# The last 64 queries of every batch taken apart: attention-times-V in 64-column tiles, in front of the next batch's scores

## The chip, the core and the metric

The kernel runs on one core of one Trainium2 chip. The metric is device time in microseconds (us), the median of several executions; lower is better. The engines are named as in the profile: PE (TensorE matmul; PEld is its weight load), DVE (VectorE), ACT (ScalarE), POOL (GpSimd) and SP (SyncE, which here only issues DMAs).

## What is computed

The reference, cut to what matters (8 batches, 8 heads, 576 positions, head dimension 64; then 4608 tokens, width 512, hidden width 2048):

```
scores = q @ k.T / sqrt(64) + bias_table[bucket(i - j)]     # per batch and head, 576 x 576
attn   = exp(scores - max); attn /= sum(attn)
x      = attn @ v                                           # heads side by side: 4608 x 512
h      = x @ w_in                                           # 4608 x 2048
g      = h + sin(alpha * h)**2 / alpha
out    = g @ w_out                                          # 4608 x 512
```

The bias is constant beyond a distance of 128, so the kernel multiplies the exponentials by a table only in a band around the diagonal.

## The kernel before

**Tiling.** Heads go in pairs p = 0..3, pairs in groups g = 0, 1. Keys lie on the partitions: four blocks of 128 keys (c = 0..3) and a rest of 64 keys per head, which for the two heads of a pair are put into one block of 128 rows with zeros in the other head's half (`kts`, `vhs`). The 576 queries run along the free dimension: 512 and a last 64.

**Scores of a batch** (`plan_unit`, L644). A unit is one pair of PSUM banks and one exp on ACT (L678) that reads it. Kind A is one pair of heads, one key block, queries 0 to 511: two matmuls with 64 rows each, one per head, side by side in the array. Kind B is a group's last 64 queries against the four key blocks: 16 small matmuls of 64x64. Kind C is a pair's rest of keys against all 576 queries: two matmuls of 288 columns. The exps write the tile `u` (a group; two buffers); DVE multiplies the band of `u` by the table (L703, L687, L716). `plan_att` (L723) writes out a group's order by hand: A A A, C, A A A, C, A A B, for two groups; so a batch has six stretches of 64-row matmuls on PE and 22 exps on ACT.

**AV** (`plan_av`, L839), attention times V, for a pair: the weights are `u` (keys x 128 queries), the streamed operand is V with a column of ones (65 columns), whose result is the row sum. A query tile of 128 takes nine matmuls: one of 130 columns for the rest of keys (`vh`) and eight of 65 (two heads, four key blocks). From batch 1 on a pair has two windows (`WIN`, L287): queries 0 to 383 in three tiles, and 384 to 575 in two tiles that start at 384 and 448, so that 64 queries are computed twice. Then DVE takes the reciprocal of the sums and multiplies (L885, L886) into `xn`, and `xn` is transposed into `xT`: by a DMA transpose that SP issues (L898) for the first pairs (all but the last from batch 2 on), by PE and a copy (L910, L917) for the others. From batch 2 on that is five PE transposes a batch.

**Batch 0** is special: its windows are 256, 256 and 64 queries (`WIN0`, L288), and its last 64 queries are done in batch 1: `plan_late` (L777) makes the B units into a tile `ut`, and `plan_tail` (L792) the AV with weights of 64 columns, two pairs side by side in the array, 18 matmuls per group. POOL copies the rest-of-keys part of `u` into `ut` (L690).

**The second half**, per block b of 512 tokens: `plan_moe_in` (L926) makes 16 tiles h (four matmuls of 512 columns each, "w_in" below), sin on ACT (L950), a square on ACT or DVE (L957, L959), and on DVE the sum that gives g (L964). `plan_mo` (L996) multiplies g by w_out: four groups of 16 matmuls of 512 columns ("w_out" below), each group in one PSUM bank (6 or 7), copied to `outs` by DVE or ACT (L537, L539) and stored by an SP DMA (L1018). Block b starts when the queries it needs of batches b-1 and b are in `xT`. Exp and sin need different ACT tables, so there are two table loads a batch (L1025).

**The order.** `Plan.run` (L148) is a planner that runs while the kernel is built: each task has an engine, a cost, a priority and dependencies, and the planner emits the task that can start first. The 64 w_out matmuls of a block are its filling: they have the lowest priority (`fill`) and go where PE would wait, up to a quota during the scores (`QUOTA`, L211). On the chip each engine runs its own stream in the emitted order and waits by semaphores. PSUM banks 0 to 5 go to scores (in pairs), h and transposes; 6 and 7 to AV and w_out.

Of the kernel before, what the change touches and what calls it, by code (L numbers as in the profile page):

```python
# [32 lines left out]
D_TBL = 1.285  # L33
LAT = {"PE": 0.2, "ACT": 0.18, "DVE": 0.18, "POOL": 0.2, "SP": 2.4}
NBUF = {"u": 2, "g": 2, "s16": 3, "sq": 3, "outs": 5, "xn": 6}
# [175 lines left out]
QUOTA = 48  # L211
QUOTA1 = 44
# [4 lines left out]
T_KEEP = 20.0  # L217
# [14 lines left out]
T_LD = 33.0  # L232
AV0 = 1200
# [31 lines left out]
def kernel(  # L265
# [21 lines left out]
    WIN = ((0, 384), (384, 192))  # L287
    WIN0 = ((0, 256), (256, 256), (512, 64))  # L288
# [72 lines left out]
    def new_u():  # L361
        return tp.tile([128, 2, 9, S], F16, name="u", tag="u", bufs=NBUF["u"])

# [162 lines left out]
    ut = nat1x[:, 0 : NP * 9 * 64].rearrange("p (h k q) -> p h k q", h=NP, k=9)  # L526
    utb, udone = Buf("ut"), {}
# [116 lines left out]
    def plan_unit(t, g, p, kind, c, u, ub, done, gate, base):  # L644

        b, sc, mark = Buf("sc"), Cell(), plan.add({}, None)
        y = p - 2 * g
        b.users.append(mark)

        def qk(e):  # L650
            sc.v = bank(b, 2)
            kT, qT = kTs[t % 2], qTs[t % 2]
            if kind == "C":
# [13 lines left out]

        def ex(e):
            if kind == "A":
                o = u.v[:, y, 0:8, :].rearrange("p (z c) q -> p z c q", z=2)[:, :, c, 0:512]  # L670
                x = sc.v
            elif kind == "B":
                o = u.v[:, :, 0:8, 512:S] if t else ut[:, 2 * g : 2 * g + 2, 0:8, :]
                x = sc.v.rearrange("p z (c y q) -> p y (z c) q", c=4, y=2)
            else:
                o = u.v[:, y, 8, :].rearrange("p (b q) -> p b q", b=2)
                x = sc.v[:, :, 0:288]
            nc.scalar.activation(out=o, in_=x, func=AF.Exp, scale=0.125)  # L678

        n = 576 if kind == "C" else 1024  # L680
        x = plan.add({"ACT": n / 1200.0 + 0.065}, ex, [mark] + gate, base + 20, use=[b, ub])
        late = 0.0 if t else T_MH if kind == "C" else T_M2[p]
        if kind == "C":

            def bd(e):
                io = u.v[:, y, 8, 384:S]
                k_of(e).tensor_tensor(out=io, in0=io, in1=mh[:, p, 0:192], op=ALU.mult)  # L687

            def keep(e):
                nc.gpsimd.tensor_copy(out=ut[:, p, 8, :], in_=u.v[:, y, 8, 512:S])  # L690

            done[(p, "C", 0)] = x
            d = done[(p, "C", 1)] = plan.add(
                {"POOL": 0.6} if t == 0 and p else {"DVE": 0.19}, bd, [x], base + 10, nb=late, use=[ub])
            if t == 0:
                udone[(p, "C")] = plan.add({"POOL": 0.25}, keep, [d], base + 10, nb=T_KEEP, use=[ub])
# [13 lines left out]
        else:  # L710

            def bd(e):
                io = u.v[:, :, 0:8, 512:S] if t else ut[:, 2 * g : 2 * g + 2, 0:8, :]
# [4 lines left out]
            d = plan.add({"DVE": 0.25}, bd, [x], base + 10, nb=late, use=[ub])  # L718
            for pp in (2 * g, 2 * g + 1):
                done[(pp, "B", 0) if t else (pp, "B")] = d  # L720
        return b, mark, qk, x

    def plan_att(t, g, gates, first, gate):  # L723
# [6 lines left out]
        if t == 0:  # L730
            runs = [[x] for r in runs for x in r if x[1] != "B"]
        exps, head = [], []
        n_run = 0
        for i, units in enumerate(runs):
            base = PB + 3200 * g + (600 * i if t else 300 * i)
            made = [plan_unit(t, g, *x, u, ub, done, gate, base + 30 * k)
                    for k, x in enumerate(units)]
            deps = list(gates)
            for p, kind, _ in units:
                for pp in ((a, b) if kind == "B" else (p,)):  # L740
                    if t < 2:
                        deps += tr[(t, pp, 0)][1 if kind == "C" else 0] + tr[(t, pp, 1)][0]

            def run(e, i=i, made=made):
                if i == 0:
                    if g == 0:
                        first()
                        plan.in_qk, plan.used = True, 0
                        plan.quota = QUOTA1 if t == 1 else QUOTA
                    u.v = new_u()  # L750
                plan.share = (g * len(runs) + i + 1) / (2 * len(runs))
                if g == 1 and i == len(runs) - 1:
                    plan.in_qk = False
                for x in made:
                    x[2](e)

            if units[0][1] == "C":
                d, ends = 0.245, [0.245]
            else:
                ends = [0.1 + 0.2185 * (k + 1) for k in range(len(units))]  # L760
                d = ends[-1] + 0.11
            m = plan.add({"PE": d}, run, deps, base, after=head,
                         new=([ub] if i == 0 else []) + [x[0] for x in made],
                         use=[] if i == 0 else [ub])
            m.pad = () if t else (256,)
            m.offs = ([0.0] if i == 0 else []) + [0.1 + 0.2185 * k for k in range(len(units))]
            m.marks = [(x[1], o) for x, o in zip(made, ends)]
            head = [m]
            exps += [x[3] for x in made]
        for p in (a, b):  # L770
            for w in range(2):
                i = (2, 4)[w] if p == a else 4
                base = PB + 3200 * g + 600 * i + 50 * w
                xdone.setdefault((t, w), []).extend(plan_av(t, g, p, w, u, ub, done, base))
        return exps

    def plan_late(base, gate):  # L777

        made = [plan_unit(0, g, 2 * g, "B", 0, None, utb, udone, gate, base + 30 * g) for g in range(2)]
# [5 lines left out]
        m = plan.add({"PE": 0.65}, run, pe_gate, base, new=[x[0] for x in made])  # L785
        m.offs = [0.1, 0.32]
        m.marks = [(x[1], o) for x, o in zip(made, (0.32, 0.54))]
        for g in range(2):
            plan_tail(g, base + 1200 + 100 * g)
        return [x[3] for x in made]  # L790

    def plan_tail(g, base):  # L792
        ab, xb, tb = Buf("av"), Buf("xn"), Buf("h")
        av, xn, tr_ = Cell(), Cell(), Cell()
        us = [udone[(2 * g + y, k)] for y in range(2) for k in "CB"]

        def mm(e):
            av.v = bank(ab)
            for k in range(9):
                for y in range(2):  # L800
                    p, r = 2 * g + y, slice(64 * y, 64 * y + 64)
                    if k == 0:
                        full(av.v[r, 0 : 2 * VC], ut[:, p, 8, :], vhs[0][:, p, :], True, False)
                        continue
                    z, c = (k - 1) // 4, (k - 1) % 4
                    full(av.v[r, VC * z : VC * z + VC], ut[:, p, 4 * z + c, :],
                         vs[0][:, c, 2 * p + z, :], False, k == 8)

        x = plan.add({"PE": 0.5}, mm, us, base, new=[ab], use=[utb])

        def norm(e):
            x = av.v[:, 0 : 2 * VC].rearrange("p (z d) -> p z d", z=2)
            xn.v, rd = new_xn(), new_rd()
            r = rd[:, 0:2]
            nc.vector.reciprocal(out=r, in_=x[:, :, D])
            nc.vector.tensor_tensor(
                out=xn.v[:, 0].rearrange("p (z d) -> p z d", z=2), in0=x[:, :, 0:D],
                in1=r.unsqueeze(2).to_broadcast([128, 2, D]), op=ALU.mult,
            )

        x = plan.add({"DVE": 0.47}, norm, [x], base, new=[xb], use=[ab])

        def turn(e):
            tr_.v = bank(tb).bitcast(F16)
            nc.tensor.transpose(out=tr_.v[:, 0:128], in_=xn.v[:, 0], identity=id_sb)

        x = plan.add({"PE": 0.06}, turn, [x], base, new=[tb], use=[xb])

        def put(e):
            copy_on(e, xT[:, 2 * g : 2 * g + 2, 512:S],  # L830
                    tr_.v[:, 0:128].rearrange("p (y q) -> p y q", y=2))

        xdone.setdefault((0, 2), []).append(plan.add(
            {"DVE": t_dve(128), "ACT": t_act(128) + 0.03}, put, [x], base, use=[tb]))

    QC = ((0, 128, 256), (384, 448))
    QC0 = ((0, 128), (256, 384))

    def plan_av(t, g, p, w, u, ub, done, base):  # L839

        q0, n = (WIN if t else WIN0)[w]
        QS = (QC if t else QC0)[w]
        nq = len(QS)
        y = p - 2 * g
        ab, xb, tb = Buf("h" if t == 0 and p == NP - 1 and w else "av"), Buf("xn"), Buf("h")
        av, xn = Cell(), Cell()
# [260 lines left out]
```

## Time and profile before

| | us |
|---|---|
| median of 3 runs (382.63 to 382.76) | 382.65 |
| the profiled execution's own time | 383.65 |
| its span, first to last instruction | 381.8 |
| PE busy, of the span | 373.5 |
| ACT busy | 313.5 |
| DVE busy | 266.9 |
| POOL busy | 92.9 |

The profile is of one execution. Its page gives busy times, a digit row per engine (40 equal slices of the span, busy share in tenths), the chain of work that ended last, and groups of equal instructions. The mean time of one matmul is a latency: matmuls are pipelined, so what one costs in a stream is the distance between starts, which the timeline shows. Batch 1's scores begin at 53.3 us, and from 77 us to 321 us the batches 2 to 7 repeat: from one set of three PE transposes to the next there are 41.5 us for the first of these periods and 40.5 to 40.6 us for each of the next five. The last stretch (from 321 us) holds two blocks of the second half.

### The profile page before, as it was taken

The numbers are of one execution on the slowest core, as the hardware profiler recorded it, in microseconds if no ns is written. First come the engines' busy times: TensorE is split into PE (matmuls) and PEld (weight loads), VectorE is DVE, ScalarE is ACT, GpSimd is POOL, SyncE is SP. The second block draws the span as 40 slices with busy tenths as digits, with TensorE's granted clock in tenths as the row PEclk, the third lists the DMA queues.
The fourth block names the chain that finished last, engine by engine and source line by source line (L and its number), as shares of the span: only waits on it lengthen the run. The fifth ranks groups of instructions, "written<-read, shape, count | busy, mean of one in ns | idle before, by whom it ended". The sixth has DMA issues, their size and how long they took to land.

```text
span 381.8 us, 8975 instructions
## 1 busy us (share of the span) xinstructions
PE 373.5 (98%) x3578; PEld 204.2 (53%) x3578; DVE 266.9 (70%) x590; ACT 313.5 (82%) x432; POOL 92.9 (24%) x136
## 2 busy tenths in 40 slices
PE   8899999999999999999999999999999999999995
PEld 4365445654465445785564456544677456444442
DVE  4496976769676967697668867796769676999000
ACT  2978999869997999799987999699979997998111
POOL 7477350046000550037000900073005000000000
PEclk9979999999999999999999999999999999999999
DMA  9989999299912999279927991699629522000212
GB/s 170 177 160 196 203 154 134 56 162 116 89 53 74 151 120 121 79 130 113 137 60 123 103 165 44 105 147 139 78 75 155 60 53 74 6 2 1 77 63 82
DMA packets 148106, 40.16 MB, mean 105 GB/s; under 512 B 136200, under 2 KB 142432, under 8 KB 148064
## 3 DMA queue, kind: packets, MB, share of 16 engines
q0 software_dynamic: 96032, 17.67, 57.3%
q1 hardware_dynamic: 51856, 21.84, 25.1%
q8 instruction: 28, 0.46, 0.5%
q14 instruction: 14, 0.11, 0.1%
q10 hardware_dynamic: 176, 0.09, 0.1%
HBM read 37.73 MB, written 16.56 MB: 142 GB/s over the span
## 4 chain that ended last, share of the span: by engine, by line
PE 89%; ACT 5%; DMA 2%; DVE 2%; issue 1%; ACTq 0%; DVEq 0%; SPq 0%
PE pb L454 89%; ACT s L950 2%; DMA m2r<-e_dram 1%; ACT u L678 1%; DMA e_dram<-e_sb 1%; ACT sq L957 1%; PE pb L910 1%; ACT qT L537 0%; DVE u L703 0%; DVE xn L886 0%; DVE sq L959 0%; DVE outs L539 0%; DVE kT L539 0%; DVE g L964 0%; ACT xT L537 0%
## 5 line engine op out<-in xcount | busy, mean ns | idle before, releaser
L678 ACT ACTIVATE u<-pb 128x1024 f16<-128x1024 f32 (+1 forms) x174 | 152.7, 962 | 12.8 <-PE pb L454 12.0
L454 PE MATMUL pb<-w_out,g 128*128 128x512 f16 x576 | 138.9, 380 | 0.2 <-DVE outs L539 0.2
L454 PE MATMUL pb<-xT,w_in 128*128 128x512 f16 (+4 forms) x704 | 127.7, 340 | 0.0
L950 ACT ACTIVATE s<-pb,alphaT 128x512 f16<-128x512 f32 x144 | 92.9, 685 | 15.4 <-PE pb L454 15.2
L964 DVE SCALAR_TENSOR_TENSOR g<-sq,inv_a,pb 128x512 f16<-128x512 f16 x144 | 101.3, 743 | 3.8 <-ACT sq L957 2.3
L454 PEld LDWEIGHTS <-w_in 128*128 128x128 f16 x704 | 64.1, 98 | 55.9
L703 DVE TENSOR_TENSOR u<-u,m2r 128x512 f16<-128x512 f16 (+1 forms) x128 | 62.4, 497 | 35.0 <-ACT u L678 31.4
L454 PEld LDWEIGHTS <-g 128*128 128x128 f16 x576 | 53.0, 98 | 60.1 <-issue 8.1
L454 PEld LDWEIGHTS <-u 128*128 128x128 f16 x1404 | 55.5, 99 | 10.9 <-issue 3.2
L454 PE MATMUL pb<-v,u 128*128 128x65 f16 x1248 | 55.3, 195 | 0.2 <-DVE u L703 0.2
L399 POOL COPY kt<-kT 64x256 f16<-64x256 f16 x12 | 5.6, 464 | 182.9 <-DMA kT<-staged_k 182.7
L454 PE MATMUL pb<-qT,kT 64*128 64x64 f16 (+1 forms) x512 | 42.8, 288 | 0.4 <-ACT u L678 0.2
L959 DVE TENSOR_TENSOR sq<-s 128x512 f16<-128x512 f16 x81 | 34.3, 425 | 11.1 <-ACT s L950 10.2
L957 ACT ACTIVATE sq<-s 128x512 f16<-128x512 f16 x63 | 39.8, 631 | 0.9
L454 PE MATMUL pb<-vh,u 128*128 128x130 f16 x156 | 34.9, 224 | 0.0
L886 DVE TENSOR_TENSOR xn<-pb,rd 128x256 f16<-128x256 f32 (+1 forms) x64 | 30.9, 482 | 2.4 <-DVE rd L885 0.3
L537 ACT ACTIVATE outs<-pb 128x512 f32<-128x512 f32 x15 | 9.0, 597 | 28.1 <-PE pb L454 28.1
L454 PEld LDWEIGHTS <-kT 64*128 64x128 f16 x512 | 16.7, 94 | 24.5 <-issue 16.6
L404 POOL DMA_DIRECT2D v<-in_v_dram x28 | 24.8, 898 | 4.7 <-DMA nat<-in_q_dram 2.4
L1025 ACT ACT_TABLE_LOAD x15 | 19.2, 1283 | 0.3
L885 DVE RECIPROCAL rd<-pb 128x4 f32<-128x4 f32 (+1 forms) x64 | 11.9, 185 | 10.8 <-PE pb L454 9.7
L539 DVE COPY outs<-pb 128x512 f32<-128x512 f32 x21 | 14.5, 689 | 4.1 <-PE pb L454 4.0
(77 smaller groups left out, 168.7 us busy)
## 6 DMA issues: line engine op xcount, KB each, us to landing
out_dram<-outs SPq DMA_DIRECT2D x36, 256.0 KB, 2.3
v<-in_v_dram POOLq DMA_DIRECT2D x28, 128.0 KB, 4.4
staged_k<-in_k_dram POOLq DMA_DIRECT2D x6, 576.0 KB, 8.2
staged_q<-in_q_dram POOLq DMA_DIRECT2D x6, 576.0 KB, 12.0
w_in<-in_moe_w_in_dram POOLq DMA_DIRECT2D x4, 512.0 KB, 7.8
w_out<-in_moe_w_out_dram POOLq DMA_DIRECT2D x4, 512.0 KB, 15.1
xT<-xn SPq DMA_TRANSPOSE x60, 2.3
w_out<-in_v_dram SPq DMA_DIRECT2D x6, 128.0 KB, 4.8
```

Of the source, the lines that this page charges most:

```text
L404: nc.gpsimd.dma_start(out=vs[t % 2][:, c, :, 0:D], in_=vp[128 * c : 128 * c + 128],)
L454: nc.tensor.matmul(out=out, lhsT=lhsT, rhs=rhs, start=start, stop=stop)
L539: k_of(e).tensor_copy(out=o, in_=i)
L678: nc.scalar.activation(out=o, in_=x, func=AF.Exp, scale=0.125)
L703: nc.vector.tensor_tensor(out=io, in0=io, in1=m2[:, 2 * p : 2 * p + 2, x0 : x0 + hi - lo], op=ALU.mult)
L885: nc.vector.reciprocal(out=r, in_=x[:, :, :, D])
L886: nc.vector.tensor_tensor(out=xn.v[:, 0:nq].rearrange("p c (z d) -> p c z d", z=2), in0=x[:, :, :, 0:D], in1=r.unsqueeze(3).to_broadcast([ ...
L950: nc.scalar.activation(out=s16.v, in_=h.v, func=AF.Sin, scale=alphaT[:, f : f + 1])
L957: nc.scalar.activation(out=sq.v, in_=s16.v, func=AF.Square)
L959: k_of(e).tensor_tensor(out=sq.v, in0=s16.v, in1=s16.v, op=ALU.mult)
L964: nc.vector.scalar_tensor_tensor(out=gcell[b].v[:, f, :], in0=sq.v, scalar=inv_a[:, f : f + 1], in1=h.v, op0=ALU.mult, op1=ALU.add,)
L1025: nc.scalar.preload_act_table_set(name)
```

## The change

All batches now do their last 64 queries as batch 0 did, with changes to where they are put.

- `u` has 512 queries instead of 576. The last 64 queries of a batch go into a tile `ut` of their own, one of two halves by the batch's parity.
- Kind C covers 512 queries, and from batch 1 on two pairs at once (two matmuls of 512 columns, one exp of 1024). A new kind X covers all pairs' rest of keys against the last 64 queries (four matmuls of 64 columns in one bank, one exp of 256).
- A batch's order from batch 1 on is written out over both groups (`plan_att`); it still has six stretches of 64-row matmuls, and 21 exps.
- AV of queries 0 to 511 is in a stretch of three tiles (0 to 383) per pair, and one tile (384 to 511) per pair, two pairs together in one bank, one normalization and one DMA transpose; there are no overlapping tiles. From batch 2 on only the last pair's three tiles are transposed by PE.
- AV of the last 64 queries of batch t-1 (36 matmuls with weights of 64 columns, for all four pairs, in one row) is emitted right ahead of the first scores of batch t, as part of the same task; for batch 0 in batch 1 and for batch 7 it is a task of its own (`tail_alone`).
- Constants: `QUOTA` 48 to 44, `QUOTA1` 44 to 32. POOL's copies into `ut` are gone.

The diff, cut to its core:

```diff
 def plan_unit(...):
+        two = kind == "C" and t > 0
+            if kind == "X":
+                for pp in range(NP):
+                    full(sc.v[:, 64 * pp : 64 * pp + 64], kts[t % 2][:, pp, :], qT[:, pp, 512:S], True, True)
+                return
             if kind == "C":
                 for z in range(2):
-                    full(sc.v[:, z, 0:288], kts[t % 2][:, p, :],
-                         qT[:, p, 288 * z : 288 * z + 288], True, True)
+                    if two:
+                        full(sc.v[:, z, :], kts[t % 2][:, p + z, :], qT[:, p + z, 0:512], True, True)
+                    else:
+                        full(sc.v[:, z, 0:256], kts[t % 2][:, p, :],
+                             qT[:, p, 256 * z : 256 * z + 256], True, True)
...
-    def plan_att(t, g, gates, first, gate):
-        runs = ([(a, "A", 0), (a, "A", 1), (a, "A", 2)], [(a, "C", 0)],
-                [(a, "A", 3), (b, "A", 0), (b, "A", 1)], [(b, "C", 0)],
-                [(b, "A", 2), (b, "A", 3), (b, "B", 0)])
+    def plan_att0(g, gates, gate):
...
+    def plan_att(t, gates, gate):
+        A = [(p, "A", c) for p in range(NP) for c in range(4)]
+        runs = (A[0:3], [(0, "C", 0)], A[3:6], A[6:9], A[9:12], [(2, "C", 0)], A[12:15],
+                A[15:] + [(0, "B", 0), (2, "B", 0)], [(0, "X", 0)])
...
+            tl = plan_tail(t - 1, base) if i == 0 and t > 1 else None
+            def run(e, i=i, made=made, tl=tl, fresh=fresh):
...
+                if tl:
+                    tl[0](e)
+                for x in made:
+                    x[2](e)
...
+        for p in range(NP):
+            plan_av(t, [(p, 128 * i) for i in range(3)], *us[p // 2], done, bases[(2, 3, 5, 7)[p]],
+                    p < (2, NP - 1)[t > 1])
+        for g in range(2):
+            ps = [[2 * g, 2 * g + 1]] if g == 0 or t > 1 else [[2], [3]]
+            for x in ps:
+                plan_av(t, [(p, 384) for p in x], *us[g], done,
+                        bases[(4, 7)[g]] + 50 if g == 0 or t == 1 else PB + AV_LATE, g == 0 or t > 1)
...
+    def tail_alone(t, base):
+        tl = plan_tail(t, base)
+        m = plan.add({"PE": D_TAIL + 0.1}, tl[0], tl[1], base, new=[tl[2]], use=[tl[3]])
...
-    def plan_tail(g, base):
+    def plan_tail(t, base):
         def mm(e):
             av.v = bank(ab)
-            for k in range(9):
-                for y in range(2):
+            for g in range(2):
+                x0 = 2 * VC * g
+                for k in range(9):
+                    for y in range(2):
+                        p, r = 2 * g + y, slice(64 * y, 64 * y + 64)
...
+        if t:
+            def turn(e):
+                for y in range(2):
+                    nc.sync.dma_start_transpose(
+                        out=xT[:, y::2, x0 : x0 + 64],
+                        in_=xn.v[64 * y : 64 * y + 64, 0:2].rearrange("p c d -> p (c d)"),
+                    )
...
+        if t == T - 1:
+            tail_alone(t, PB + 10015)
```

The emitted order of PE in a period changes with it (w_in is 64 matmuls, M counts w_out matmuls, A A A is six 64-row matmuls, v27 are three query tiles of AV, X a PE transpose, T36 the new set of 36, A B B one A and two B units):

```
before: w_in M12 AAA M3 C M8 AAA M3 C M2 v27 M2 AAB M9 AAA v27 C M5 v18 AAA M1 v18 C M3 v27 AAB M11 v27 M5 X3 v36 w_in(X2 after its first 8)
after:  w_in M17 T36 AAA M3 C M8 AAA M6 v27 AAA M9 AAA v27 C M4 v18 AAA M1 v27 M3 ABB M3 X-scores M3 v27 M6 X3 v18 M1 w_in
```

More of the change, by code (lines that the diff above doesn't have):

```diff
@@ L232 @@
 T_LD = 33.0
+AV_LATE = 9000
 AV0 = 1200
@@ L685, in bd @@
             def bd(e):
[L686 to L696, printed above, removed]
+                io = ut[:, :, 8, :]
@@ new lines, in bd @@
+                nc.vector.tensor_tensor(out=io, in0=io, in1=mh[:, :, 128:192], op=ALU.mult)
+            done["X"] = plan.add({"DVE": 0.25}, bd, [x], base + 10, use=[ub])
+        elif kind == "C":
+            ys = slice(0, 2) if two else slice(y, y + 1)
+            def bd(e):
+                io = u.v[:, ys, 8, 384:512]
+                k_of(e).tensor_tensor(
+                    out=io, in0=io, in1=mh[:, 2 * g + ys.start : 2 * g + ys.stop, 0:128], op=ALU.mult
+                )
+            d = plan.add({"POOL": 0.45} if t == 0 and p else {"DVE": 0.25 if two else 0.15}, bd, [x],
+                         base + 10, nb=late, use=[ub])
+            for pp in (p, p + 1) if two else (p,):
+                done[(pp, "C", 0)], done[(pp, "C", 1)] = x, d
@@ L753, in run @@
                     plan.in_qk = False
+                x[2](e)
+            d, ends = run_time([unit + (False,)])
+            m = plan.add({"PE": d}, run, deps, base, after=head,
+                         new=([ub] if i == 0 else []) + [x[0]], use=[] if i == 0 else [ub])
+            m.pad = (256,)
+            m.offs = ([0.0] if i == 0 else []) + [0.1]
+            m.marks = [(x[1], ends[0])]
+            head = [m]
+            exps += [x[3]]
+        for p in (a, b):
+            for w in range(2):
+                base = PB + 3200 * g + 600 * ((2, 4)[w] if p == a else 4) + 50 * w
+                plan_av(0, [(p, 256 * w), (p, 256 * w + 128)], u, ub, done, base, False)
@@ L754, in run @@
                 for x in made:
                     x[2](e)
[L757 to L765, printed above, removed]
@@ L766, in plan_att @@
-            m.offs = ([0.0] if i == 0 else []) + [0.1 + 0.2185 * k for k in range(len(units))]
-            m.marks = [(x[1], o) for x, o in zip(made, ends)]
+            d, ends = run_time([x + (True,) for x in units])
+            d0 = D_TAIL if tl else 0.0
+            m = plan.add({"PE": d0 + d}, run, deps + (tl[1] if tl else []), base, after=head,
+                         new=([tl[2]] if tl else []) + new + [x[0] for x in made],
+                         use=use + ([tl[3]] if tl else []))
@@ L781, in run @@
+        units = [(0, "B", 0), (2, "B", 0), (0, "X", 0)]
+        made = [plan_unit(0, *x, None, tb, done, gate, base + 30 * k) for k, x in enumerate(units)]
         def run(e):
@@ L783, in run @@
                 x[2](e)
[L785 to L789, printed above, removed]
-        return [x[3] for x in made]
-    def plan_tail(g, base):
+        m = plan.add({"PE": 0.78}, run, pe_gate, base, new=[tb] + [x[0] for x in made])
+        m.offs = [0.0, 0.1, 0.32, 0.6]
+        m.marks = [(x[1], o) for x, o in zip(made, (0.32, 0.54, 0.78))]
@@ L809, in plan_tail @@
[L809 to L834, printed above, removed]
@@ L905, in plan_av, with made @@
-        tr_, x1 = Cell(), QS[0]
+            xn.v = new_xn()
+            norm_av(av.v, xn.v, nq)
+        x = plan.add({"DVE": 0.4 + 128 * nq / 960.0}, norm, prev, base + (NORM_PRI if t else NORM0),
+                     new=[xb], use=[ab])
+        x0 = S * t % XN + q0
+        two = parts[-1][0] > p0
+        def made(x):
+            rows = S * t + q0, S * t + parts[-1][1] + 128
+            xdone.append((t, rows, p0, x))
+        if dma:
+            def turn(e):
+                o = (xT[:, p0 : p0 + 2, x0 : x0 + 128] if two else
+                     xT[:, p0, x0 : x0 + 128 * nq].rearrange("d (c q) -> d c q", c=nq))
+                nc.sync.dma_start_transpose(
+                    out=o, in_=xn.v[:, 0:nq].rearrange("p c d -> p (c d)"))
+            made(plan.add({"SP": 0.3}, turn, [x], base, use=[xb]))
+            return
@@ L1046 @@
                 tr[(0, p + 1, kq)] = plan_tr(0, p + 1, kq, (150, 650, 5)[p], T_PAIR[p][kq])
-        for g in range(2):
-            if t == 1 and g == 1:
+        if t == 0:
+            for g in range(2):
+                exps += plan_att0(g, pe_gate, gate)
+        else:
+            exps += plan_att(t, pe_gate, gate)
+            if t == 1:
                 exps += plan_late(PB + LATE, gate)
-            exps += plan_att(t, g, pe_gate, first, gate)
         if t == 0:
@@ L1066 @@
             plan.add({"SP": 5.5}, turn_in, [], PB + 9000, after=tbl + [
-                x for w in range(2) for x in xdone[(t, w)] if "SP" in x.engs])
+                x for tt, _, _, x in xdone if tt == t and "SP" in x.engs])
+        if t == T - 1:
+            tail_alone(t, PB + 10015)
         sins = []
```

258 lines of the change are left out of this document (153 added, 105 removed).

## The prediction, made before the changed kernel was run

> **What bounds the kernel now.** I read the page's busy times and slices first, then the chain of work that ended last, then busy time by stretch for the repeating batches.
>
> ```profile
> PE 373.5 (98%) x3578; PEld 204.2 (53%) x3578; DVE 266.9 (70%) x590; ACT 313.5 (82%) x432; POOL 92.9 (24%) x136
> PE   8899999999999999999999999999999999999995
> PE 89%; ACT 5%; DMA 2%; DVE 2%; issue 1%; ACTq 0%; DVEq 0%; SPq 0%
> ```
> ```profile
> 158.92:199.56 40.64, 40.64 (x452) 26.67 (x450) 30.70 (x68) 36.20 (x48) 10.34 (x11) 1.00 1.00 111
> 199.56:240.04 40.48, 40.48 (x389) 21.40 (x386) 30.60 (x68) 36.20 (x48) 10.31 (x11) 1.00 1.03 111
> ```
> In the second fence the first number after a stretch is its length; then come PE, PEld, DVE, ACT and POOL busy, the granted clock and the DMAs. PE is busy in all of it, at a granted clock of 1.00, ACT 36.2 us of 40.5. A busy PE can still hide small waits behind a pipelined matmul's latency; I take those from distances between starts, below. So a period is the sum of PE's stream plus PE's small waits. What PE issues less of comes off, as long as ACT (4.3 us idle a period) does not become the loop.
>
> **PE prices.** Distances between starts in the timeline:
>
> ```profile
> 53.33 0.82 PE L454 MATMUL pb<-qT,kT 64*128 64x512 f16 x6
> 54.08 0.25 PE L454 MATMUL pb<-vh,nat 128*64 128x130 f16 x2
> 54.16 0.42 PE L454 MATMUL pb<-v,nat 128*64 128x65 f16 x16
> 54.51 0.39 PE L454 MATMUL pb<-w_out,g 128*128 128x512 f16 x1
> ...
> 142.11 0.22 PE L454 MATMUL pb<-vh,u 128*128 128x130 f16 x1
> 142.16 0.41 PE L454 MATMUL pb<-v,u 128*128 128x65 f16 x8
> 142.41 0.22 PE L454 MATMUL pb<-vh,u 128*128 128x130 f16 x1
> ```
> An AV tile of nine matmuls costs 142.41 - 142.11 = 0.30 us. Batch 0's tail in the old kernel (18 matmuls with 64-column weights) took 54.51 - 54.08 = 0.43 us with the way out of that shape: the 2 of 130 columns 0.08, then eight pairs at 0.03 each, then 0.12 to the next matmul where 0.03 is the pair: 0.095 is the change of shape. The two of a pair start 0 to 7 ns apart, so they run side by side. The same 0.095 is at each change to and from the 64-row scores (w_out to scores 0.311 instead of 0.2155, and back 0.308 instead of 0.213).
>
> **The change on PE, part by part.**
> 1. AV tiles: batches 1 to 7 lose 4 of 20 tiles: 28 x 0.30 = -8.40 us.
> 2. Tails. A set of 36 streams 2 x (0.077 + 8 x 0.030) = 0.635. Ahead of scores it adds one change of shape (the change into the scores is there anyway): 0.73, six times. Batch 0's set lies between an A run and C and batch 7's among w_in: 0.82 each. The old tail of batch 0 cost 2 x 0.43 + 2 x 0.093 = 1.05. Together 6 x 0.73 + 2 x 0.82 - 1.05 = +4.97.
> 3. PE transposes: 58 before, 44 after by the built order; three take 0.17 (118.27 to 118.44 in the timeline), so 14 x 0.056 = -0.78. What replaces them are DMAs: SP's transposes into xT fall from 60 to 47, and the two for a tail are issued early in the batch, about 20 us before the block that reads them. The rows give 2.3 us to landing and 1.2 us of SP each. The copies after the PE transposes also shrink (ACT and DVE, off the path).
> 4. Last keys: 64 matmuls of 288 columns at 0.1215 = 7.78 before. After: 28 of 512 at 0.2155, 8 of 256 at about 0.109 (an estimate from the 288 row), 32 of 64 at 0.029 (the B units' pace): 7.83. Nothing.
> 5. Stretches of 64-row matmuls: 57 in both orders, so their changes of shape stay. w_in (704) and w_out (576) stay.
>
> Sum: -8.40 + 4.97 - 0.78 + 0.05 = **-4.16 us**; per repeating period -1.20 + 0.73 - 0.11 = -0.58.
>
> **The TensorE rule against this.** "TensorEngine Tiling (Array Packing)", section Restrictions and Gotchas, of the Trainium skill says that column tiling excludes the fast weight load. "TensorE: Matmul & The Clock Gate" of the Trainium skill, section Part 3: Packing small matmuls, adds that a weight load overlaps running matmuls only where the row group differs, which these do not. By that rule the 36 loads would stand on the path, and the change would lose; the rows at 54.16 (16 matmuls, 16 loads, 0.35 us) show no such cost. It is the last rival below.
>
> **PE's waits.** In one old period (199.56 to 240.04) distances over the stream and the changes of shape add up to 0.43 us: 0.12 and 0.09 where C follows three w_out, 0.07 inside an A run, 0.05 and 0.09 ahead of AV tiles. In the new order I followed one period by hand with these rows. A run's first exp starts 0.43 to 0.46 after the run (136.33 to 136.79, 139.93 to 140.36), an exp of 1024 adds 0.94 on ACT (six and one C take 6.22, three and one C 3.40), and the pair is free 1.07 after its exp's start (136.79 to 137.86). The third unit of a run comes 0.43 after its first. From the start of the first A run: C waits 0.1 for the first exp; the second run's third unit waits 0.14 for C's exp, which now is 1024 wide (0.94 instead of 0.58); the fourth run 0.09, the fifth 0.12, ABB 0.2 if none takes up another's. Added up 0.65, with one taking up part of another about 0.5. AV tiles do not wait: each one's last band product on DVE ends at least 0.2 us earlier by these rows, and bank 6 or 7 is normalized or copied 0.05 to 0.6 us before its next use. So +0.1 per period, +0.6 in six; bounds -0.43 (no waits at all) and +0.6 (each of six runs loses 0.2). Batch 1's 1.56 us of waits (0.64 of it between two pairs of transposes at 79.24, 0.36 at 56.3) I leave as they are: the new order fills some places with w_out and w_in and adds a longer chain of transposes at the end; bounds -1.3 and +1.0. Up to 50 us the orders agree almost one by one: nothing, bounds ±0.5 (the low clock of 16 to 24 us makes a delay there dearer).
>
> **Other engines.** ACT: 22 exps become 21, 18 x 0.94 + 4 x 0.58 = 19.24 before and 20 x 0.94 + 0.31 = 19.11 after; a copy of `outs` (0.60) goes to DVE, which has 30.6 of 40.5 busy. Cover: after its last exp and the table load at 156.92 (1.28) ACT waited until 161.28 for the first sin, 3.1 us with one copy in it. PE from the first A run to w_in takes 23.64 before; after, by the new order and the prices, 21.95. So about 1.4 us of ACT's cover are left there, and about 1.8 ahead of the first exp, where PE now has M17 T36 instead of M12. What is queued behind T36 are the scores and so the exps; this cover pays for it. POOL loses four small copies; the loads of kT, qT and V sit where they did (kT and qT had landed at about 211, scores at 217.4).
>
> **Forecast.** -4.16 + 0.6 = -3.56. The profiled execution took 383.65 us (span 381.8 and 1.85 around it): 380.1 on that footing. It is 1.0 above the median of the runs, 382.65; the times shown are of such runs, so 382.65 - 3.56 = **379.1 us**. What a measurement of this kernel can tell from no change is about 0.2%, 0.8 us.
>
> **Rivals.**
> - *ACT's releases eat part of it.* The chance is in the 0.12 to 0.2 waits of the A runs' third units, in 5 runs where the old order had one. If all show in full and batch 1's chain of transposes costs 1.0: -4.16 + 3.6 x 0.4 + 1.0 + 0.2 = -1.5, so 381.1. For: C's exp is 1.6 times as long. Against: the second and third run leave ACT idle (0.36 us by hand), which lets PE catch up.
> - *More than forecast.* Batch 1's waits are filled (-1.3) and the periods' waits stay at 0.43: -4.16 - 1.3 = -5.5, so 377.2. For: w_out matmuls stand in those places in the new order.
> - *No net change*: the waits come to 0.6 more in each of seven batches: 382.7.
> - *Slower: ACT becomes the loop, and T36 is where PE feels it.* T36 writes bank 6, whose w_out group ends with the third of the M17, and DVE copies that bank only behind the last g of the block. In the old trace the last g ends at 136.71, 3.06 after w_in's end (133.65); plus a copy of 0.69 and a signal of 0.06 that is 3.81, and T36 comes after 17 x 0.2155 + 0.095 = 3.76. It is level: every 0.1 us by which the sins come later against w_in is a 0.1 us wait of PE, with all scores behind it. It decides the sign from about 2.0 us: 1.4 of cover at the first sin and 0.58 of gain. At 2.5 us, 1.1 + 0.05 a period: -4.16 + 6 x 1.15 = +2.7, so 385.4. For: it is level. Against: in the new order DVE has one normalization ahead of a block's first squares, where it had two.
> - *The 64-column loads are not hidden*: 36 loads at the mean of their row in the groups (LDWEIGHTS from `nat`, 128x64, x36: 111 ns) are 4.0 instead of 0.63, seven sets more: +23.6 - 3.6, so 402.7. The batch-0 rows speak against it.
>
> **Chances.** Forecast (378.0 to 380.2) 0.62; eaten (380.2 to 381.9) 0.16; more (below 378.0) 0.09; no net change 0.05; slower by ACT 0.07; loads 0.01. Within 0.2% (381.9 to 383.4): 0.05; slower 0.08; faster 0.87. The range of 8 in 10 takes the forecast, most of "eaten" and the nearer half of "more": 377.4 to 381.2.
>
> **What would show it.** Right: periods of 39.9 to 40.1 us from one set of three transposes to the next; T36 in 0.63 us with 0.095 ahead; 44 PE transposes; PE still busy throughout and ACT idle near 1.8 us ahead of the first exp. Wrong: waits over 0.2 in front of A runs' third units (ACT's releases); T36 more than 3.9 us behind w_in's last start (the slower rival); pairs of T36 over 0.05 apart (the loads); the first w_in of a block waiting for SP's transposes into xT, which I cost at nothing because they are issued over 3 us ahead.

## The result and the profile after

The changed kernel takes **378.68 us** (median of 4 runs, 378.32 to 378.94), the kernel before on the same chip 382.7 us (382.63 to 382.76): a ratio of 0.9894 (95% interval 0.9877 to 0.9911). The forecast was 379.1, the range 377.4 to 381.2. The profiled execution took 378.73 us, 377.0 of it span.

The page of the changed kernel: busy times, slices, and the chain's shares by engine.

```profile
PE 367.7 (98%) x3568; PEld 195.7 (52%) x3568; DVE 260.7 (69%) x563; ACT 311.8 (83%) x426; POOL 91.7 (24%) x132
...
PE   8889899999999999999999999999999999999995
...
PEclk9999999999999999999999999999999999999999
...
PE 87%; DMA 6%; ACT 3%; POOL 2%; SPq 1%; issue 0%; DVE 0%; ACTq 0%
```

PE lost 5.8 us of busy time at the same 98%, and its slices are as full as before: PE is still the bound, and less work on it became less time. Two repeating periods, from the first scores of a batch to those of the next, in the view by stretch (length; PE, PEld, DVE, ACT, POOL; clock; DMA):

```profile
170.87:210.90 40.03, 40.01 (x389) 20.45 (x385) 30.25 (x65) 35.38 (x46) 10.54 (x12) 1.00 1.06 117
210.90:250.92 40.02, 40.00 (x387) 20.43 (x384) 30.21 (x65) 35.38 (x46) 10.15 (x11) 1.00 1.00 113
```

The period went from 40.48 to 40.03 us. ACT is at 35.38 of it (36.2 before), so it has not become the loop. The new set of 36 stands here in PE's timeline (start, duration from the first start to the last end, operation):

```profile
206.39 3.83 PE L453 MATMUL pb<-w_out,g 128*128 128x512 f16 x17
210.15 0.25 PE L453 MATMUL pb<-vh,nat 128*64 128x130 f16 x2
210.23 0.42 PE L453 MATMUL pb<-v,nat 128*64 128x65 f16 x16
210.48 0.23 PE L453 MATMUL pb<-vh,nat 128*64 128x130 f16 x2
210.54 0.42 PE L453 MATMUL pb<-v,nat 128*64 128x65 f16 x16
210.90 0.82 PE L453 MATMUL pb<-qT,kT 64*128 64x512 f16 x6
```

From its first start to the next scores it is 210.90 - 210.15 = 0.745 us; its first start is 0.309 after the last w_out's, which is a w_out and the change of shape (0.2155 + 0.095) with no wait for the bank. No DVE or ACT stands in the brackets behind these lines: PE waited for nobody there.

Where the time went, by stretches of the two profiled executions (first scores of a batch to first scores):

| stretch | before | after | difference |
|---|---|---|---|
| start to batch 1's first scores | 53.33 | 52.40 | -0.93 |
| batch 1 | 42.53 | 38.42 | -4.11 |
| batches 2 to 6 | 202.72 | 200.30 | -2.42 |
| batch 7 to the end | 83.22 | 85.88 | +2.66 |

The second and fourth rows must be read together: batch 1 issues 49 w_out matmuls instead of 62 in that stretch, and the last stretch 194 instead of 180, and each is 0.2155. From batch 1's first scores on the gain is 3.87 us, of which one w_out (0.22) is work that the changed kernel has done earlier: 15 of the 576 stand ahead of batch 1's first scores, where it was 14. The 0.93 ahead of them cannot be put down to the change. The row of the granted clock in the page of before has a 7 in its third slice, the row of after, above, has none (means up to batch 1 of 0.94 and 1.00):

```profile
PEclk9979999999999999999999999999999999999999
```

And e1 below runs the old code up to there, at a clock of 1.00, and begins batch 1 at 52.30. The medians, which differ by 4.02, are the better measure.

### The profile page after: what moved, and what is told of

Same layout as the page of the kernel before. It is cut to its first block, busy times and chain, and to the rows that moved or that the text cites. A ratio compares the mean times of both kernels' runs of the same rounds, so it can differ in the third digit from the quotient of the medians.

```text
span 377.0 us, 8905 instructions
## 1 busy us (share of the span) xinstructions
PE 367.7 (98%) x3568; PEld 195.7 (52%) x3568; DVE 260.7 (69%) x563; ACT 311.8 (83%) x426; POOL 91.7 (24%) x132
## 4 chain that ended last, share of the span: by engine, by line
PE 87%; DMA 6%; ACT 3%; POOL 2%; SPq 1%; issue 0%; DVE 0%; ACTq 0%
PE pb L453 86%; DMA nat<-in_q_dram 3%; ACT u L692 3%; DMA w_out<-in_v_dram 1%; DMA e_dram<-e_sb 1%; POOL w_in L434 1%; PE pb L555 1%; POOL v L418 0%; SPq L469 0%; PE pb L1009 0%; SPq L476 0%; POOL u L709 0%; POOL nat L428 0%; ACT outs L536 0%; ACT e_sb L594 0%
## 5 line engine op out<-in xcount | busy, mean ns | idle before, releaser
L692 ACT ACTIVATE u<-pb 128x1024 f16<-128x1024 f32 (+1 forms) x146 | 136.0, 1020 | 15.7 <-PE pb L453 15.3
L453 PEld LDWEIGHTS <-u 128*128 128x128 f16 x1152 | 44.4, 97 | 9.4 <-issue 2.8
L453 PE MATMUL pb<-v,u 128*128 128x65 f16 x1024 | 44.5, 193 | 0.2 <-ACT u L692 0.2
L1060 ACT ACTIVATE sq<-s 128x512 f16<-128x512 f16 x66 | 41.5, 637 | 1.2 <-DVE g L1067 0.3
L1062 DVE TENSOR_TENSOR sq<-s 128x512 f16<-128x512 f16 x78 | 32.6, 426 | 14.0 <-ACT s L1053 12.9
L938 DVE TENSOR_TENSOR xn<-pb,rd 128x256 f16<-128x256 f32 (+2 forms) x59 | 28.5, 483 | 2.0
L453 PE MATMUL pb<-vh,u 128*128 128x130 f16 x128 | 28.2, 220 | 0.3 <-DVE xn L938 0.2
L536 ACT ACTIVATE outs<-pb 128x512 f32<-128x512 f32 x10 | 6.0, 597 | 23.2 <-PE pb L453 23.2
L937 DVE RECIPROCAL rd<-pb 128x4 f32<-128x4 f32 (+2 forms) x59 | 11.0, 187 | 16.0 <-PE pb L453 15.1
L538 DVE COPY outs<-pb 128x512 f32<-128x512 f32 x26 | 17.9, 687 | 3.6 <-PE pb L453 3.6
```

What stands on the lines that cost most here:

```text
L453: nc.tensor.matmul(out=out, lhsT=lhsT, rhs=rhs, start=start, stop=stop)
L538: k_of(e).tensor_copy(out=o, in_=i)
L937: nc.vector.reciprocal(out=r, in_=x[:, :, :, D])
L938: nc.vector.tensor_tensor(out=xn[:, 0:n].rearrange("p c (z d) -> p c z d", z=2), in0=x[:, :, :, 0:D], in1=r.unsqueeze(3).to_broadcast([128 ...
L1060: nc.scalar.activation(out=sq.v, in_=s16.v, func=AF.Square)
L1062: k_of(e).tensor_tensor(out=sq.v, in0=s16.v, in1=s16.v, op=ALU.mult)
```

## The experiments

Twelve kernels ran. Medians of before in the three groups and the last run were 382.46 (e1 to e4), 383.21 (e5 to e8), 382.52 (e9 to e11) and 382.79 (e12). Periods are of batches 4 and 5, from first scores to first scores.

### e1: the old order with one part of the change

The kernel before, with its second windows transposed by DMA from batch 2 on: three PE transposes a batch instead of five.

```diff
-        if p < (0, 2, NP - 1)[min(t, 2)]:
+        if p < (0, 2, NP - 1)[min(t, 2)] or (t > 1 and w):
```

> The old kernel with one part of the change alone: from batch 2 on the last pair's second window (queries 384 to 575) is transposed by SP's DMAs instead of by two PE transposes. PE's emitted order is otherwise the same. Theory (the gain is what PE issues less of, at its price in the stream): 12 transposes x 0.056 = -0.67 us in all, the repeating period 40.48 to 40.37 us. Rival (the gain comes from the new order and its waits, single PE instructions do not count one for one): no change, period 40.48.

Measured: 382.18 us, ratio 0.9987 (0.9974 to 0.9999); period 40.37 instead of 40.48:

```profile
216.10:256.47 40.37, 40.37 (x384) 21.35 (x384) 30.41 (x68) 36.20 (x49) 9.50 (x11) 1.00 1.04 111
```

Two transposes at 0.056 come out of the period one for one, and the added DMAs cost nothing that shows.

### e2: the two halves of the array one after the other

```diff
-                for k in range(9):
-                    for y in range(2):
+                for y in range(2):
+                    for k in range(9):
```

> The changed kernel with the same 36 tail matmuls in another order: for each group first the 18 of one column half, then the 18 of the other, so that two neighbours no longer fall on different halves of the array. Theory (the side-by-side halves are what makes a tail cheaper than the overlapping tiles): a set goes from 0.63 to about 4 x 0.30 = 1.20 us, +0.57 in each of 8, +4.5 us in all, so about the old kernel's time (383.2); period 40.03 to 40.6. Rival (the gain is in the order, fewer exps and DVE work): under +0.5 us. Third: the array pairs them whatever their order: no change.

Measured: 380.62 us, ratio 0.9945 (0.9925 to 0.9966); period 40.35, +0.325 instead of the +0.57 expected. PE's timeline of e2 shows why it is less:

```profile
210.66 0.24 PE L453 MATMUL pb<-vh,nat 128*64 128x130 f16 x1
210.74 0.32 PE L453 MATMUL pb<-v,nat 128*64 128x65 f16 x5
210.88 0.24 PE L453 MATMUL pb<-vh,nat 128*64 128x130 f16 x1
210.90 0.38 PE L453 MATMUL pb<-v,nat 128*64 128x65 f16 x8
211.09 0.24 PE L453 MATMUL pb<-vh,nat 128*64 128x130 f16 x1
```

At the pace of an AV tile nine matmuls of one half would take 0.30 alone, but each half's first (the line of 130 columns) starts 0.215 after the other's: it runs beside the last ones of the half before, though it was issued after them. In the trace's single starts the second half's first follows a matmul of the first half by 6 ns. So the set takes 0.94 from its first start to its last instead of 0.62: issuing the two halves in turn, matmul by matmul, is worth about 0.33 a set here. What no overlap at all would cost, this run does not show.

### e3: four matmuls instead of 36

Of the nine steps of the set only the first is issued. Waits, banks, DMAs and normalization stay.

```diff
-                for k in range(9):
+                for k in range(1):
```

> The changed kernel with the tails' AV left out but for the rest of the keys: 4 matmuls of 130 columns in the place of 36 (the last 64 queries of each batch then see only the last 64 keys). Theory: the set goes from 0.63 to about 0.13 us, 0.5 x 8 = -4.0 us, 374.7 us; period 39.5. Rival (ACT's loop is close behind PE): the period falls by clearly less than 0.5, and the waits ahead of the third units of the A runs grow.

Measured: 375.61 us, ratio 0.9816 (0.9793 to 0.9839); period 39.52, -0.51:

```profile
207.31:246.84 39.53, 39.51 (x357) 19.93 (x353) 30.21 (x65) 35.37 (x46) 10.15 (x11) 1.00 1.02 116
```

The set's stream stands on the path one for one, and nothing else was late behind it.

### e4: the set as a task of its own

```diff
-            tl = plan_tail(t - 1, base) if i == 0 and t > 1 else None
+            tl = None
+            if i == 1 and t > 1:
+                tail_alone(t - 1, bases[2] + 10)
```

> The changed kernel with each batch's tail as a task of its own that the planner may put anywhere in the batch, instead of as the head of the scores' task. In the emitted order it falls right behind the first w_in matmuls' stretch, with w_out on its other side, mostly. Theory (the place is worth one change of shape): +0.095 x 6 = +0.6 us and up to 0.3 of other waits; period 40.03 to 40.1 or 40.2. Rival (the place ahead of the scores carries the gain): back to about the old period, 40.5.

Measured: 384.02 us, ratio 1.0035 (1.0022 to 1.0048): slower than before, 5.3 above the changed kernel, far more than either theory gave. Ahead of the scores of batches 3 to 5 the planner, free to choose, put the set right behind w_in, and only three w_out between it and the scores:

```profile
126.42 0.25 PE L453 MATMUL pb<-vh,nat 128*64 128x130 f16 x2
...
127.17 0.82 PE L453 MATMUL pb<-w_out,g 128*128 128x512 f16 x3
127.92 0.60 PE L453 MATMUL pb<-qT,kT 64*128 64x512 f16 x4
128.78 0.37 PE L453 MATMUL pb<-qT,kT 64*128 64x512 f16 x1 [0.25 <-DVE g L1069]
129.44 0.37 PE L453 MATMUL pb<-qT,kT 64*128 64x512 f16 x1 [0.29 <-DVE g L1069]
129.99 0.59 PE L453 MATMUL pb<-w_out,g 128*128 128x512 f16 x2 [0.18 <-DVE xn L940]
```

The brackets name the releaser: PE's scores wait for DVE's last g, because the banks that they write still hold h. Here the bracket understates the wait, since a pipelined matmul still counts as busy: the start at 128.78 comes 0.63 after the one before it, where 0.2155 is the pace, and the bracket says 0.25. By distances between starts the first run of scores loses about 1.1 us, and the waits of batches 2 to 6 are about 7.5 us against 2.75 in the changed kernel. With six more changes of shape (0.57) that is the 5.3. Of the 4.8 us of waits, 3.6 stand at that first run and the w_out behind it in three batches; the B units of the same batches wait 0.5 longer each time for an exp. (The periods of batches 4 and 5 cannot be compared here: 38.05 and 41.98, with 48 and 65 w_out.) 50 w_out matmuls that were not used as cover run in the last stretch instead, where they cover nothing. So most of what the set's place costs is what it leaves between w_in and the first scores.

### e5 and e6: more work on ACT ahead of the sins

One and three copies of 128x1024 on ACT behind the sin table load, from batch 1 on.

```diff
             set_table(SIN_SET)
+            for _ in range(1 if t else 0):       # e6: 3
+                nc.scalar.activation(out=ascr, in_=zz2, func=AF.Copy)
```

> The changed kernel with one more ACT copy (128x1024, fp16, SBUF to SBUF, about 0.95 us) behind each sin table load from batch 1 on; the emitted order of everything else is the same. The trace of the changed kernel shows ACT waiting 1.73 us there for PE. Theory (PE's stream is the period, ACT has cover): no change, 378.7 us, period 40.03, the wait of the first sin 0.8. Rival (ACT is the loop): +0.9 in each of 6 periods, +6 us.

> The same with three copies (about 2.8 us). Theory (the slower rival of the prediction, with its point): the first sin comes 1.1 us later than PE's w_in allows, the last g 1.1 later, DVE's copy of bank 6 behind it too, and the tail, whose start has 0.17 us to spare against that copy, waits 0.9; period 40.9, +5 to +6 us in all, though ACT still has 2.2 us to spare ahead of the first exp. Rival (only ACT's sum counts: 4.65 us idle a period): no change.

Measured, e5: 379.15 us, ratio 0.9904 (0.9882 to 0.9927), period 40.03, unchanged. ACT's timeline of the changed kernel, and of e5, in two of the steady periods:

```profile
190.62 1.28 ACT L1128 ACT_TABLE_LOAD   x1
193.64 0.69 ACT L1053 ACTIVATE s<-pb,alphaT 128x512 f16<-128x512 f32 x1 [1.73 <-PE pb L453]
```
```profile
232.01 1.06 ACT L1167 ACTIVATE ascr<-zz 128x1024 f16<-128x1024 f16 x1
233.73 0.69 ACT L1056 ACTIVATE s<-pb,alphaT 128x512 f16<-128x512 f32 x1 [0.66 <-PE pb L455]
```

The bracket is ACT's idle time ahead of the first sin: 1.73 without and 0.66 with the copy, 1.07 less, and the copy takes 1.06. The cover took it whole.

Measured, e6: 387.3 us, ratio 1.0116 (1.0087 to 1.0146). The steady period is 40.56, +0.53. The copies exceed the cover by 3.23 - 1.73 = 1.5; the sins come 1.41 later against w_in, some of that is made up in the stretch of sins, where ACT otherwise waits 0.17 to 0.24 for PE (the last sin ends 0.74 later), and the set of 36 waits 0.53. The other periods cost more, +2.36, +2.46 and +2.13 from batch 1 on, which neither theory gave: there the block's last PE transposes are copied into `xT` by ACT, and that copy stands behind the copies that I put in. ACT, then PE, in e6:

```profile
115.38 3.23 ACT L1167 ACTIVATE ascr<-zz 128x1024 f16<-128x1024 f16 x3
118.52 0.47 ACT L539 ACTIVATE xT<-pb 128x384 f16<-128x384 f16 x1
```
```profile
119.04 4.26 PE L455 MATMUL pb<-xT,w_in 128*128 128x512 f16 x19 [2.30 <-ACT xT L539]
```

A delay on ACT had two ways to PE, and the one I had not seen, through `xT` to w_in, has less cover: e5's one copy costs 0.18, 0.28 and 0.00 in the same three periods, so of 3.23 us it takes up about 0.8 to 1.1.

### e7: the old quotas

```diff
-QUOTA = 44
-QUOTA1 = 32
+QUOTA = 48
+QUOTA1 = 44
```

> The changed kernel with the old kernel's two quotas (48 and 44 instead of 44 and 32), which move where w_out matmuls are put. Theory (only what PE issues counts): within 0.4 us of 378.7, period 40.0 to 40.1. Rival (the gain comes from the placing of w_out): over +1 us.

Measured: 379.29 us, ratio 0.9903 (0.9887 to 0.9919); the period is 40.25 (+0.22), but more w_out is done before the last stretch (from batch 7's first scores to PE's last start it is 78.5 us, where the changed kernel has 81.7), and the total cannot be told from the changed kernel's. The constants are not where the gain comes from.

### e8 and e10: fewer PE transposes

From batch 2 on (e8), and in batch 1 for three of four pairs too (e10), all transposes by DMA.

```diff
-                    p < (2, NP - 1)[t > 1])
+                    p < (2, NP)[t > 1])          # e10: (NP - 1, NP)
```

> The changed kernel with the last three PE transposes of a batch, from batch 2 on, also given to SP's DMAs: 18 fewer. The order puts w_out and AV between the last pair's AV and the next w_in, so the DMA (2.4 us to landing) has about 3.5 us. Theory: -18 x 0.056 = -1.0 us, 377.7 us, period 39.86. Rival (the landing takes the place of the transposes): the first w_in of a block waits for SP's transposes into xT, and the period stays at 40.0 or grows.

> The kernel without PE transposes from batch 2 on, and in batch 1 pair 2's three tiles by DMA as well. Theory (PE's stream): 3 x 0.056 = -0.17 us against that kernel, 377.0, if the landing of 2.4 us is covered by w_out in batch 1. Rival (batch 1 ends on that chain): the first w_in of block 1 waits for SP, +0.5 us or more.

Measured: e8 377.19 us, ratio 0.9841 (0.9823 to 0.9859), period 39.745, -0.285 instead of -0.17: three transposes at 0.056 are 0.17, and the waits fell from 0.49 to 0.39 a period. e10 376.37 us, ratio 0.9836 (0.9815 to 0.9856), not to be told from e8. The last pair's DMA transpose is not late for w_in in the repeating periods.

### e9: the set ahead of the second run of scores

```diff
-            tl = plan_tail(t - 1, base) if i == 0 and t > 1 else None
+            tl = plan_tail(t - 1, base) if i == 2 and t > 1 else None
```

> The changed kernel with the tail at the head of the second stretch of A units (third run of the written order) instead of the first, so that it again shares one change of shape with scores; w_out stays ahead of the first scores. Theory A (the place among the scores is indifferent, and the loss of the tail as a task of its own came from w_out no longer covering the wait for the last g ahead of the first scores): period 39.9 to 40.2, total within 0.5 us of the changed kernel. Theory B (the place ahead of the first scores is what gains): period over 40.5, total +3 us or more.

Measured: 377.61 us, ratio 0.9868 (0.9846 to 0.989); period 39.84, -0.18 (batch 5; batch 4 takes 39.63 with one w_out fewer). In the stream the same matmuls cost the same (T36 0.75); the wait of 0.19 inside the B units is gone; the planner now has four w_out ahead of them instead of three. A place ahead of the first scores is not needed; with e4, what is needed there is the cover.

### e11 and e12: both at once

e11 is e8 and e9 together.

> No PE transposes from batch 2 on and the tail at the head of the second stretch of A units. Theory A: period 39.7 to 39.8 as without PE transposes alone, about 377.2 us. Theory B: period over 40.2.

Measured: 383.12 us, ratio 1.0012 (0.9999 to 1.0026), 5.9 us above e8, with periods of 40.90. I had expected the two gains to add up. In one period PE's waits are 1.57 us (e8 0.39, e9 0.34), and PE's timeline shows where:

```profile
225.32 0.40 PE L453 MATMUL pb<-v,u 128*128 128x65 f16 x8
225.56 0.59 PE L453 MATMUL pb<-qT,kt 128*128 128x512 f16 x2
225.99 0.38 PE L453 MATMUL pb<-w_out,g 128*128 128x512 f16 x1
226.60 0.22 PE L453 MATMUL pb<-vh,u 128*128 128x130 f16 x1 [0.23 <-DVE xn L938]
...
227.29 0.61 PE L453 MATMUL pb<-qT,kT 64*128 64x512 f16 x4
228.06 0.39 PE L453 MATMUL pb<-qT,kT 64*128 64x512 f16 x2 [0.16 <-ACT u L692]
```

Two stretches of AV that use one bank stand with C and a single w_out between them, so the second waits for DVE's normalization of the first (0.395 by distances between starts), and the scores behind it for an exp. In e8 and e9 four w_out stand there; the planner's order had shifted. e12 changes one constant of e11 that brings those four back in batches 2 to 6:

```diff
-QUOTA1 = 32
+QUOTA1 = 40
```

> Run before this one: the two cuts together (no PE transposes from batch 2 on, and the set of 36 ahead of the second run of scores) took 383.1 us, 1.0012 of the kernel before, with periods of 40.90 us and 1.57 us of waits of PE in each, where each cut alone had 39.74 and 39.84 with 0.39 and 0.34. In its trace the largest waits stand where the planner's order had put one w_out matmul, instead of four, between two AV stretches that use the same bank: 0.395 us for DVE's normalization of the first (226.60), then 0.32 in the next run of scores, and 0.18 and 0.41 at the end of the batch. This kernel changes one constant of it, QUOTA1 from 32 to 40, by which the planner's order again has M6 v27 .. C M4 v18 M1 in place of M8 v27 .. C M1 v18, in batches 2 to 6, and the last two blocks' w_out together. Theory (the cover between AV stretches is what was lost): the waits go back to 0.3 to 0.5 a period, the period to 39.7 to 39.9, the time to 376.5 to 378. Rival (the two cuts collide in themselves, on SP's queue or on DVE, whatever the order): the period stays at 40.6 to 40.9 and the time at 382 to 383.

Measured: **375.48 us**, ratio 0.9809 (0.9788 to 0.9831). The same place in e12:

```profile
223.25 0.59 PE L453 MATMUL pb<-qT,kt 128*128 128x512 f16 x2
223.68 1.03 PE L453 MATMUL pb<-w_out,g 128*128 128x512 f16 x4
224.54 0.22 PE L453 MATMUL pb<-vh,u 128*128 128x130 f16 x1
```

Its period in the view by stretch:

```profile
211.32:250.93 39.61, 39.61 (x382) 20.17 (x382) 29.41 (x64) 36.09 (x48) 10.06 (x12) 1.00 1.04 117
```

The second stretch of AV starts 0.86 behind the first w_out, four times 0.2155, and waits for nothing. The period is 39.61, with 0.26 of waits; the waits of batches 2 to 6 fell from 7.30 to 1.43. The five periods fell by 5.8 of the 7.6 us (four of them by 1.29 each, batch 2's by 0.60); the rest lies outside these periods, where the constant changes the order as well (the two last blocks' w_out now stand together), and I did not take it apart. The collision of the two cuts was in the order, not in the cuts. e12 beats both kernels; its ratio is the lowest of all, though its interval overlaps those of e8 and e10.

## Why the prediction was right, step by step

The time, its sign and its mechanism came out as forecast; that the number came so close is in part luck. The sum of the stream was -4.16; with the waits as measured (batch 1: 1.56 to 1.00; batches 2 to 6: 2.12 to 2.75; batch 7: 0.43 to 0.49, together +0.13) and the one w_out done earlier (-0.22) that is -4.25, against -3.87 measured from batch 1's first scores on. So 0.38 of the stream's gain did not come, some 0.05 in each of seven batches, and I did not trace it; batch 1's waits, forecast at nothing, gave 0.56 and hid it.

1. *AV tiles, transposes, last keys.* The period's -0.58 of stream, with 0.1 more of waits, was to give -0.48, and gave -0.45. With the 0.06 of waits that came, the stream gave -0.51. That PE's stream converts one for one is shown by e1 (-0.11 for two transposes) and e3 (-0.51 for 32 matmuls). The largest term, the AV tiles, was not run alone; it rests on the timelines, where a tile takes 0.30 and a period has 16 instead of 20. There are 44 PE transposes.
2. *The set of 36.* Forecast 0.73, with one change of shape. The change from w_out takes 0.31 from start to start whether the set or the scores come next, so the set's net cost is the 0.745 from its start to the scores (0.617 to its last start, 0.128 from there). The second group's first pair costs 0.057, not 0.077: only the first pair behind the change of shape was dearer.
3. *The 64-column loads.* The groups give 36 loads at a mean of 111 ns, 4.0 us a set if they stood in line; the set takes 0.62. The rule of the Trainium skill, "TensorE: Matmul & The Clock Gate", section Part 3: Packing small matmuls, by which a weight load overlaps running matmuls only where the row group differs, does not hold by itself in this trace: all of these loads use all rows, and the pairs start every 0.026 to 0.033 us. (The same section of the Trainium skill also lets a load into the background weight buffer go ahead of running matmuls; whether that is what happens here, no run shows.)
4. *The waits.* 0.1 more a period was forecast, 0.06 came, and at the places of the list that the prediction made by hand: C 0.095 (0.1 forecast), the third units of the second, fourth and fifth run 0.05, 0.09 and 0.06 (0.14, 0.09 and 0.12), and that of A B B, which is the second B unit, 0.19 (0.2). Batch 1's waits, left at nothing with the bounds "-1.3 and +1.0", came to -0.56: this is the term that was missed. It is more than the 0.3 by which the traced gain was larger than forecast; the part of the stream that did not come took some of it back.
5. *ACT's cover.* Forecast 1.4 us ahead of the first sin and 1.8 ahead of the first exp; measured 1.73 (above) and 2.17:

```profile
211.33 2.85 ACT L692 ACTIVATE u<-pb 128x1024 f16<-128x1024 f32 x3 [2.17 <-PE pb L453]
```

6. *"It is level"*, of the bank that the set waits for, was too dark: DVE's copy ended at 209.89, the set began at 210.15.

```profile
207.89 1.40 DVE L1067 SCALAR_TENSOR_TENSOR g<-sq,inv_a,pb 128x512 f16<-128x512 f16 x2
209.21 0.68 DVE L538 COPY outs<-pb 128x512 f32<-128x512 f32 x1
```

One sign of being wrong was set off by a matmul. The set begins 3.97 us behind w_in's last start, and the sign said 3.9; but one w_in, 17 w_out and the change of shape are 18 x 0.2155 + 0.095 = 3.97 without any wait. The 3.76 that the sign was built on counts from w_in's end.

The rival "slower by ACT" was right as a mechanism and wrong in its price and its place. Its price: sins that come 1.41 us later cost 0.53 a steady period (e6), not 1.4. Its place: the nearer one is the copy into `xT`, in the batches where ACT makes it. By e5 the changed kernel takes 1.06 us more on ACT without a change of its steady period.

What I had not weighed at all is the planner. I costed what PE issues, and took the order as built. e4 adds no matmul and e11 even takes some away, and they cost 5.3 us against the changed kernel and 5.9 against e8, more than the change gained: in e4 but for the changes of shape, and in e11 as e12 shows, by where w_out matmuls stand.

## What to carry to other kernels

Where one engine is busy throughout at a constant clock, price a change by distances between starts in the timeline, not by mean times of instructions: the terms that could be read alone (the set, a pair of transposes) came out within 0.02 us, the stream of a period within 0.07. Then look at what the independent work (here w_out) covers: a matmul taken from between two users of one bank, or from between a producer's end and the first reuse of its banks, can cost more than the time it takes. In e11 three w_out, 0.65 us, were missing at one place, and PE waited 0.395 there and 0.32 in the scores behind. With a planner, compare the built order at these places after every edit, even one that only removes work.

## What the runs showed of the hardware

- Matmuls of two column halves overlap even if they are issued nine by nine (e2: 0.215 us between the halves' starts, where an AV tile of nine takes 0.30).
- ACT's next instruction began 0.01 us after the end of the table load (e5: the load from 230.72 takes 1.28, the copy begins at 232.01). The Trainium skill, "ScalarE: Activation LUTs", section What ACT_TABLE_LOAD costs, gives a drain of about 1.38 us on top of 1.283; the load's time agrees; the drain shows on neither side of the load (the exp before it ends at 230.70).
- Two profiled executions can differ by 1 to 1.5 us in a stretch in which PE's instructions are the same. Up to batch 1's first scores the kernel before took 53.33 at a mean granted clock of 0.94, and e1 took 52.30 at 1.00; but the changed kernel took 52.40 and e3 50.85, both at 1.00, so the clock is not the whole of it.
